# The first channel product by seven block products, with the sums of its weights kept in DRAM

## The chip, the cores and the metric

The kernel runs on one core of one Trainium2 chip. Its time is the device time of one execution in microseconds; the kernel before has a median of 951.89 us over three runs (951.26 to 952.92).

## The reference

Eight batches, eight heads, 576 positions, head size 64. An attention stage makes x (batch, 576, 512), and a mixer works on it:

```python
# attention, for each batch and head
q_d, k_d, v_d = means over 4 neighbouring positions        # 144 positions
out_up    = repeat(softmax(q_d k_d^T / 8) v_d, 4)
out_local = softmax(q k^T / 8 where |i - j| < 4) v
x = out_up + out_local                                      # (576, 512) per batch
# mixer
h  = relu(x^T @ w_tok1) @ w_tok2                            # 576 -> 256 -> 576
u  = x + h^T                                                # (576, 512)
h2 = relu(u @ w_ch1) @ w_ch2                                # 512 -> 1536 -> 512
return u + h2
```

The two products of the last line but one are called the first and the second channel product here; they hold most of the arithmetic.

## The kernel before

**Numbers.** Each factor of a product in the mixer is kept as two float16 parts, a rounded value and its remainder. A product of two such factors is three matmuls (`mm3`, line 119: value by value, value by remainder, remainder by value), accumulated in float32 in a PSUM bank. The names in the profile: `uh` is u as two parts, `CW` and `CX` are the parts of w_ch1 and w_ch2, `c` is a bank of either channel product, `h` the hidden activations as two parts.

**Tiles.** Everything is transposed, so that channels lie on partitions and positions on the free axis. The 576 positions are cut into two chunks of 256 and 320. For a chunk the first product (`first`, line 788) makes 12 tiles of 128 hidden channels, each from four blocks of 128 input channels by three matmuls: 12 matmuls a tile. `first_up` (line 803) takes each tile out of its bank with two instructions: ScalarE writes relu(c) as float16 (line 808), VectorE the remainder (line 810). The second product (`second`, line 813) sums over the 12 hidden tiles into four output tiles, 36 matmuls each, and `second_up` (line 827) adds the scaled result to u and sends it out. Three PSUM banks (`m0` to `m2`) serve both products in turn.

**Scales.** Before a chunk's first product, u is divided by a power of two that depends on its largest magnitude (`scaled`, line 717): a maximum over the tiles, a transpose and a broadcast on TensorE (`um_t`, `um_b`), three small instructions on VectorE, then for each of four blocks one instruction on ScalarE (line 730) and one on VectorE (line 732). So `uh` is ready chunk by chunk.

**Side work.** Attention and the token product (`pooled`, `local`, `mix`) of batch b+1, and the loads of batch b+2 (`ahead`), are put between the channel products of batch b: `tick` in the main loop (lines 932 to 961) lets the side work advance in proportion to the work done. `sd`, `td`, `ad` are scores, transposed exponentials and outputs of the pooled attention, `sc`, `pT`, `av` those of the local one; `x` is its result.

**Order.** Batch 0, its weights and the start of batch 1 are ordered by a planner (`drive`, line 160) from estimated costs, with the list `ORDER` (line 34) as the rule between streams that are ready together. From there the code's order holds, and the scheduler may move instructions of one engine past each other; each engine then runs its list strictly in order. SyncE issues the loads and the output transfers, ScalarE the transfer of the pooled output.

The weights of the first product stay in SBUF as 12 tiles `CW` of two parts, 128 by 512 each, from batch 0 on.

## Time and profile before

| | |
|---|---|
| median of three runs | 951.89 us (951.26 to 952.92) |
| the profiled execution | 952.87 us, of it the span of the trace 951.1 us |
| mean granted TensorE clock | 0.98 of full speed |
| TensorE matmuls busy | 96% of the span |
| VectorE, ScalarE, GpSimd busy | 52%, 35%, 24% |
| moved by DMA | 68.34 MB |

Busy shares are means over stages of different kinds: a start of some 100 us in which weights are converted, then one stretch of about 109 us for each batch, then the last batch, which has no side work beside it. The time column of a group is its busy time; "idle before" names whom the engine waited for. The 1.8 us between the span and the execution's time lie around the trace.

### The profile page before, as it was taken

What the parts mean: (1) busy time and instruction counts of PE and PEld (TensorE: products, weight loads), DVE (VectorE), ACT (ScalarE), POOL (GpSimd) and SP (SyncE); (2) the same over time, 40 slices, a digit from 0 to 9 for tenths busy, and PEclk for the clock granted to TensorE, in tenths of its full rate; (3) what the DMA queues carried; (4) which work ended last, traced back from release to release, by engine and by line L of the source; (5) the groups of instructions that cost most, each with busy time, mean ns of one, the idle gap of its engine ahead of it and who ended that gap; (6) DMA issues with size and microseconds to landing.
All of it is one profiled execution on the core that took longest, in us unless ns stands there. A gap on an engine that the chain in (4) does not pass through costs nothing.

```text
span 951.1 us, 26153 instructions
## 1 busy us (share of the span) xinstructions
PE 910.7 (96%) x11456; PEld 680.7 (72%) x11456; DVE 490.9 (52%) x1189; ACT 334.1 (35%) x732; POOL 232.1 (24%) x361
## 2 busy tenths in 40 slices
PE   8777899999999999999999999999999999999998
PEld 4444688677876788677876787677876778767876
DVE  7899987446552356325653365424563254533221
ACT  3755562424252242314242151423333143422120
POOL 4999941511330003400312004400124000000000
PEclk9977899999999999999999999999999999999999
DMA  9772404610250002600241002500124000000000
GB/s 268 199 264 81 177 21 94 185 45 16 75 159 23 21 18 72 162 16 15 70 139 42 21 17 73 168 8 22 37 71 143 15 16 26 14 1 29 12 12 28
DMA packets 28226, 68.34 MB, mean 72 GB/s; under 512 B 3504, under 2 KB 14000, under 8 KB 26864
## 3 DMA queue, kind: packets, MB, share of 16 engines
q1 hardware_dynamic: 25552, 64.30, 22.4%
q10 hardware_dynamic: 2560, 2.36, 1.0%
q8 instruction: 90, 1.47, 0.6%
q14 instruction: 24, 0.20, 0.1%
HBM read 54.85 MB, written 9.44 MB: 68 GB/s over the span
## 4 chain that ended last, share of the span: by engine, by line
PE 45%; DVE 5%; DMA 2%; ACT 1%; issue 0%; ACTq 0%; POOL 0%; SPq 0%
PE c L121 32%; PE t L121 5%; PE ad L553 2%; DMA vw<-od 2%; PE av L622 1%; PE t L686 1%; PE td L544 1%; PE pT L609 1%; PE sc L586 1%; DVE uh L732 1%; DMA vr<-in_vr_dram 1%; PE sd L525 1%; DVE P L605 1%; DVE xh L664 1%; DVE P L598 0%; DVE r L603 0%
## 5 line engine op out<-in xcount | busy, mean ns | idle before, releaser
L121 PE MATMUL c<-uh,CW 128*128 128x256 f16 (+1 forms) x2304 | 310.0, 286 | 0.0
L121 PE MATMUL c<-h,CX 128*128 128x256 f16 (+1 forms) x2304 | 308.5, 286 | 0.0
L121 PEld LDWEIGHTS <-CW 128*128 128x128 f16 x2304 | 218.1, 98 | 65.6 <-issue 6.7
L121 PEld LDWEIGHTS <-CX 128*128 128x128 f16 x2304 | 220.4, 98 | 56.5 <-issue 0.8
L810 DVE SCALAR_TENSOR_TENSOR h<-c,h 128x256 f16<-128x256 f32 (+1 forms) x192 | 87.4, 455 | 157.1 <-ACT h L808 156.5
L808 ACT ACTIVATE h<-c 128x256 f16<-128x256 f32 (+1 forms) x192 | 78.6, 409 | 189.4 <-PE c L121 188.9
L473 POOL TENSOR_TENSOR vr<-vr 72x256 f32<-72x256 f32 x64 | 49.9, 781 | 369.9 <-DVE vm L470 198.1
L836 DVE SCALAR_TENSOR_TENSOR u<-c,io,u 128x256 f32<-128x256 f32 (+1 forms) x64 | 32.9, 514 | 93.2 <-PE c L121 92.6
L711 ACT ACTIVATE u<-t,down 128x256 f32<-128x256 f32 (+1 forms) x64 | 29.9, 498 | 122.8 <-PE t L121 122.8
L713 DVE TENSOR_REDUCE umx<-u 128x1 f32<-128x256 f32 (+1 forms) x64 | 27.7, 450 | 77.1 <-ACT u L711 77.1
L121 PE MATMUL t<-xh,W 128*128 128x512 f16 (+1 forms) x240 | 61.0, 389 | 3.3 <-DVE xh L664 3.3
L499 POOL TENSOR_TENSOR qs<-qk 128x288 f32<-128x288 f32 x56 | 40.9, 730 | 93.7 <-DMA qk<-in_qk_dram 90.0
L470 DVE TENSOR_REDUCE vm<-vr 72x1 f32<-72x512 f32 x64 | 43.2, 677 | 30.5 <-DMA vr<-in_vr_dram 30.0
L121 PE MATMUL t<-W,hid 128*128 128x256 f16 (+1 forms) x384 | 58.2, 287 | 0.0
L627 ACT ACTIVATE x<-av,up 128x512 f32<-128x512 f32 (+1 forms) x40 | 27.1, 681 | 79.3 <-PE av L622 78.8
L537 ACT ACTIVATE pd<-sd,nmd 72x144 f32<-72x144 f32 x128 | 38.9, 378 | 25.5 <-DVE nmd L532 18.7
L664 DVE SCALAR_TENSOR_TENSOR xh<-x,back,xh 128x512 f16<-128x512 f32 (+1 forms) x40 | 33.7, 843 | 23.1 <-ACT xh L662 22.5
L553 PE MATMUL ad<-vd,ptd 72*72 72x65 f32 x512 | 39.4, 229 | 5.9 <-POOL vd L474 5.8
L553 PEld LDWEIGHTS ad<-vd,ptd 72*72 72x72 f32 x512 | 37.5, 145 | 8.2 <-POOL vd L474 6.7
L121 PEld LDWEIGHTS <-W 128*128 128x128 f16 (+1 forms) x240 | 22.3, 98 | 28.2 <-issue 7.8
L730 ACT ACTIVATE uh<-u,us 128x256 f16<-128x256 f32 (+1 forms) x64 | 29.8, 524 | 34.5 <-DVE us L127 23.9
L121 PEld LDWEIGHTS <-hid 128*128 128x128 f16 x384 | 34.9, 98 | 9.5 <-DVE hid L700 0.7
(129 smaller groups left out, 976.2 us busy)
## 6 DMA issues: line engine op xcount, KB each, us to landing
qk<-in_qk_dram SPq DMA_DIRECT2D x32, 579.0 KB
vw<-in_vw_dram SPq DMA_DIRECT2D x32, 351.0 KB
vr<-in_vr_dram SPq DMA_DIRECT2D x64, 144.0 KB
C_raw<-in_c_dram SPq DMA_DIRECT2D x16, 512.0 KB
out_dram<-u SPq DMA_DIRECT2D x32, 160.0 KB
...
```

Of the source, the lines that this page charges most:

```text
L121: nc.tensor.matmul(ps, lhs(a), rhs(c), start=first and i == 0, stop=last and i == 2, **kw)
L470: nc.vector.tensor_reduce(st.vm[:, i:i + 1], t, axis=AX.XY, op=ALU.max, apply_absolute_value=True)
L473: nc.gpsimd.tensor_add(t[:, 0:2], t[:, 0:2], t[:, 2:4])
L499: nc.gpsimd.tensor_add(two, x[:, :, 0:2], x[:, :, 2:4])
L537: nc.scalar.activation(pd[:, par, g], s[:, par, g], AF.Exp, bias=nm[:, par, g:g + 1], scale=0.125 / 16)
L553: nc.tensor.matmul(ps[:, g, par], pt[:, par, kg, G * g:G * g + G], st.vd[:, kg, 2 * pr + par], start=kg == 0, stop=kg == 1)
L664: nc.vector.scalar_tensor_tensor(xh[:, 1], xf(t), back[:n], xh[:, 0], ALU.mult, ALU.subtract)
L711: nc.scalar.activation(u, ps, AF.Copy, scale=st.down)
L730: nc.scalar.activation(t[:, 0], st.u[ch][c], AF.Copy, scale=s)
L808: nc.scalar.activation(ht[:, 0], ps, AF.Relu)
L810: nc.vector.scalar_tensor_tensor(ht[:, 1], ps, 0.0, ht[:, 0], ALU.max, ALU.subtract)
L836: nc.vector.scalar_tensor_tensor(us[c], banks[c], io, us[c], ALU.mult, ALU.add)
```

## The change

From batch 2 on, the first product is made for a pair of hidden tiles (a and b) and both halves of the positions at once. With A the 2 by 2 blocks of u (position half by channel half; columns of 288 positions, two blocks of 128 channels) and the weights of the pair as 2 by 2 blocks too, seven block products replace eight: a11, a12 and a22 are blocks of u, and s1 to s4 are sums and differences of them (s1 = a21 + a22, s2 = s1 - a11, s4 = a12 - s2, s3 = a11 - a21); they are multiplied by blocks of the weights or by sums of these. Each block product is two blocks of 128 channels by three matmuls of 288 columns, 42 matmuls a pair where there were 48 of 256 and 320.

The four results need partial sums of the seven products. A bank `P` takes a11, is copied (x1), takes s2, is copied (u2), takes s3, is read (m5), takes a22. A bank `R` takes s1, is copied (m5), takes s4. A bank `Q` takes a12. The copies are made by ScalarE, the additions by VectorE, then relu and remainder as before.

The sums of the weights are made in batch 1 by `weight_sums` (VectorE adds the parts, GpSimd subtracts, ScalarE and GpSimd split again), written to DRAM and read back, 0.39 MB for a pair in each batch; one of the four takes the place of a half of the weight tile `b` in SBUF. The sums of u are made on GpSimd once the whole of u is there, with one scale for both halves. The second product goes by output tile, both chunks of a tile after each other. The maxima of v become sums of squares on ScalarE. Buffers change to make room, and `ORDER` and `PX` have other values.

```diff
+    def weight_sums():
+        for p in range(NF // 2):
+            sums.append(dram.tile([128, 3, 2, 256], F16, name=f"sums{p}"))
+        for p in range(NF // 2):
+            fa, fb = C1.fin[2 * p], C1.fin[2 * p + 1]
+            y = {}
+            for n, f, o in (("a1", fa, 0), ("b1", fb, 0), ("a2", fa, 256), ("b2", fb, 256)):
+                yield step("V", 0.42)
+                y[n] = T([128, 256], F32, "tm", f"{n}_{p}")
+                nc.vector.tensor_tensor(y[n], f[:, 0, o:o + 256], f[:, 1, o:o + 256], ALU.add)
...
+            def parts(src, o):
+                nc.scalar.copy(o[:, 0], src)
+                nc.gpsimd.tensor_sub(o[:, 1], src, o[:, 0])
+
+            nc.gpsimd.tensor_sub(y["a1"], y["b1"], y["a1"])
+            nc.gpsimd.tensor_sub(y["b1"], y["b2"], y["b1"])
+            parts(y["a1"], ts12[:, 0])
+            parts(y["b1"], ts3)
+            nc.gpsimd.tensor_sub(y["b2"], y["b2"], y["a1"])
+            parts(y["b2"], ts12[:, 1])
+            nc.sync.dma_start(sums[p][:, 0:2], ts12)
+            nc.sync.dma_start(sums[p][:, 2], ts3)
+            yield step("G", 2.0, ("c1", 1, 1, 2 * p + 1))
+            nc.gpsimd.tensor_sub(y["a2"], y["a2"], y["b2"])
+            parts(y["a2"], fb[:, :, 0:256])
...
+        def mixtures():
+            yield from mixed("s1", A[1][0], A[1][1], ALU.add)
+            s = yield from scale_of(0, st.umx.rearrange("p a c -> p (a c)"))
+            st.ui[1] = st.ui[0]
+
+            def block(name, x):
+                st.uh[name] = T([128, 2, 2, HS], F16, "uh", f"{name}h{b}")
+                for i in range(2):
+                    o = st.uh[name][:, i]
+                    yield step("A", 0.5, *([("h", 1, 1, NF - 1)] if b == 2 else [("h", b - 1)]))
+                    nc.scalar.activation(o[:, 0], x[i], AF.Copy, scale=s)
+                    e = yield step("V", 0.5)
+                    nc.vector.scalar_tensor_tensor(o[:, 1], x[i], s, o[:, 0], ALU.mult, ALU.subtract)
+                make(("uh", b, name), e)
...
+    def product7(st, steps):
...
+        for p in range(NP):
+            fa, fb = 2 * p, 2 * p + 1
+            t123 = T([128, 3, 2, 256], F16, "ts", f"t123_{b}_{p}")
+            nc.sync.dma_start(t123, sums[p])
+            if P is None:
+                P = bank("m0", "P")
+                product(P, "a11", weights(fa, 0), True, False)
+                x1 = plain(P, "x1", "A")
+            Ptag, Qtag = ("m0", "m2") if p % 2 == 0 else ("m2", "m0")
+            h = T([128, 2, 2, S], F16, "h", f"h{b}_{p}")
+            R = bank("m1", "R")
+            product(R, "s1", weights(0, 0, t123, 0), True, False)
+            m5 = plain(R, "m5", "A")
+            product(P, "s2", weights(0, 0, t123, 1), False, False)
+            u2 = plain(P, "u2", "A")
+            Q = bank(Qtag, "Q")
+            product(Q, "a12", weights(fa, 1), True, True)
+            nc.vector.tensor_tensor(x1, x1, Q[:, :HS], ALU.add)
+            leave(x1, 0, 0, h)
+            product(R, "s4", weights(fb, 1), False, True)
+            nc.vector.tensor_tensor(u2, u2, R[:, :HS], ALU.add)
+            leave(u2, 0, 1, h)
+            product(P, "s3", weights(0, 0, t123, 2), False, False)
+            nc.vector.tensor_tensor(m5, m5, P[:, :HS], ALU.add)
+            leave(m5, 1, 1, h)
+            if p + 1 < NP:
+                old, P = P, bank(Qtag, "P")
+                product(P, "a11", weights(fa + 2, 0), True, False)
+                x1 = plain(P, "x1", "A")
+            else:
+                old = P
+            product(old, "a22", weights(fb, 0), False, True)
+            leave(old[:, :HS], 1, 0, h)
...
-            nc.vector.tensor_reduce(st.vm[:, i:i + 1], t, axis=AX.XY, op=ALU.max, apply_absolute_value=True)
+            nc.scalar.activation(dump, t.rearrange("p r c -> p (r c)"), AF.Square, scale=2.0 ** -20, accum_out=st.vm[:, i:i + 1])
...
-        for ch in range(2):
-            while ("uh", b, ch) not in made:
+        if b == 1:
+            for ch in range(2):
...
+                if ch == 0:
+                    work.g = together([weight_sums(), work.g], 2)
+        else:
+            while ("uh", b) not in made or ("sums",) not in made:
                 work.go()
+            g = Run(product7(st, 0))
+            while g.next is not None:
                 g.go()
+                tick(2 * S / 7)
```

In `product7`, `product` is the six matmuls of one block product, `plain` a copy of a bank by ScalarE, and `leave` the ReLU on ScalarE and the remainder on VectorE.

Three places of the order follow. **ScalarE at the start of batch 5.** Before, the eight parts of u, four for each chunk, were followed by the first ReLU of the product:

```order
L730 ACTIVATE uh5_0_0_9243<-u5_0_0_8984,us5_0_9217 128x256
L730 ACTIVATE uh5_0_1_9254<-u5_0_1_9035,us5_0_9217 128x256
L730 ACTIVATE uh5_0_2_9257<-u5_0_2_9089,us5_0_9217 128x256
L730 ACTIVATE uh5_0_3_9260<-u5_0_3_9142,us5_0_9217 128x256
L730 ACTIVATE uh5_1_0_9288<-u5_1_0_9184,us5_1_9284 128x320
L730 ACTIVATE uh5_1_1_9291<-u5_1_1_9193,us5_1_9284 128x320
L730 ACTIVATE uh5_1_2_9294<-u5_1_2_9219,us5_1_9284 128x320
L730 ACTIVATE uh5_1_3_9297<-u5_1_3_9250,us5_1_9284 128x320
L808 ACTIVATE h5_0_0_9327<-c1_5_0_0_9314 128x256
```

Now fourteen parts stand there (two each of a11, s1 and s2 are ahead of these rows), then the copies out of the banks P and R:

```order
L782 ACTIVATE a12h5_9469<-u5_2_9352,us5_0_9430 128x288
L782 ACTIVATE a12h5_9469<-u5_3_9369,us5_0_9430 128x288
L782 ACTIVATE s4h5_9474<-s45_0_9453,us5_0_9430 128x288
L782 ACTIVATE s4h5_9474<-s45_1_9454,us5_0_9430 128x288
L782 ACTIVATE s3h5_9483<-s35_0_9479,us5_0_9430 128x288
L782 ACTIVATE s3h5_9483<-s35_1_9480,us5_0_9430 128x288
L782 ACTIVATE a22h5_9488<-u5_2_9352,us5_0_9430 128x288
L782 ACTIVATE a22h5_9488<-u5_3_9369,us5_0_9430 128x288
L903 COPY x15_0_9516<-P_5_0_9509 128x288
L903 COPY m55_0_9533<-R_5_0_9526 128x288
L903 COPY u25_0_9548<-P_5_0_9509 128x288
L551 ACTIVATE pd6_0_9554<-sd6_0_9519,nmd6_0_9525 72x144 x4
```

The copy of P, which the second block product into P has to wait for, now stands behind all fourteen.

**ScalarE and TensorE in the middle of batch 4's first product.** x5_0 is the attention output of the next batch. Before, ScalarE had these rows around it:

```order
L627 ACTIVATE x5_0_8309<-av5_0_8247,up5_7696 128x2x4x64
L600 ACTIVATE P2_110<-P2_110 128x8x38
L662 ACTIVATE xh5_0_8716<-x5_0_8309,back_126 128x512
L600 ACTIVATE P0_108<-P0_108 128x8x38
L613 COPY pt5_1_8418<-pT5_1_8413 128x512
```

Now it stands among the ReLUs of a pair (h4_3) and ahead of the copy x14_3 of the next pair's bank:

```order
L908 ACTIVATE h4_3_8353<-x14_2_8341 128x288
L641 ACTIVATE x5_0_8459<-av5_0_8412,up5_7822 128x2x4x64
L908 ACTIVATE h4_3_8353<-u24_3_8406 128x288
L614 ACTIVATE P2_112<-P2_112 128x8x38
L908 ACTIVATE h4_3_8353<-m54_3_8398 128x288
L903 COPY x14_3_8520<-P_4_3_8513 128x288
```

TensorE's list at the same place, with the end of s1 and the first row of s2 of that next pair:

```order
L124 MATMUL R_4_4_8574<-s1h4_7881,t123_4_4_8571 128x288
L636 MATMUL av5_0_8412<-vw5_0_7350,pt5_0_8311 32x64 x31
L600 MATMUL sc5_3_8530<-qk5_0_7342 32x38 x8
L600 MATMUL sc5_3_8530<-qk5_1_7344 32x38 x8
L600 MATMUL sc5_3_8530<-qk5_2_7346 32x38 x8
L600 MATMUL sc5_3_8530<-qk5_3_7348 32x38 x8
L124 LDWEIGHTS t123_4_4_8571
L124 MATMUL P_4_3_8513<-s2h4_7890,t123_4_4_8571 128x288
```

The matmul into P_4_3 (s2) comes behind av5_0 and sc5_3 and needs the copy x14_3.

**VectorE in a pair of the last batch.** Where one remainder (line 810) stood for each hidden tile, a pair now has these seven rows:

```order
L937 TENSOR_TENSOR x17_0_12585<-x17_0_12585,Q_7_1_12615 128x288
L941 TENSOR_TENSOR u27_1_12613<-u27_1_12613,R_7_1_12598 128x288
L909 SCALAR_TENSOR_TENSOR h7_1_12597<-x17_0_12585,h7_1_12597 128x288
L945 TENSOR_TENSOR m57_1_12605<-m57_1_12605,P_7_0_12578 128x288
L909 SCALAR_TENSOR_TENSOR h7_1_12597<-u27_1_12613,h7_1_12597 128x288
L909 SCALAR_TENSOR_TENSOR h7_1_12597<-m57_1_12605,h7_1_12597 128x288
L909 SCALAR_TENSOR_TENSOR h7_1_12597<-P_7_0_12578,h7_1_12597 128x288
```

The third add stands behind the other two and one remainder, and it reads the bank that a22 accumulates into.

More of the change, by code (lines that the diff above doesn't have):

```diff
@@ L650, in mix @@
         NT = len(TILES)
-        st.hid, st.acc, banks, umx = [], [], {}, []
+        st.hid, st.acc, banks = [], [], {}
         def xf(t):
@@ L675, in products @@
                 make(("t1", b, t), e)
-            for ch in range(2):
+            for ch, two in WALK[b > 1]:
                 s0, N = CHUNKS[ch]
-                for c in range(4):
+                for c in (2 * two, 2 * two + 1):
                     e = yield step("P", 0.3 + N * 2.6e-3, *(("W", "y", NT + i) for i in range(4)), ("hid", b),
-                                   *([("over", b - 1, 0)] if b and ch == 0 else []), take="" if c % 2 else f"gg>{b}")
+                                   *([("over", b - 1, c - 2)] if b > 2 and c > 1 else []), take="" if c % 2 else f"gg>{b}")
                     if c % 2 == 0:
@@ L726, in scaled @@
+                s = yield from scale_of(ch, st.umx[:, ch])
                 uh = st.uh[ch] = []
@@ L738, in together @@
+        return [splits(), products(), takes(), mixtures() if b > 1 else scaled()]
     def together(todo, most):
@@ L816, in second @@
+    def second(st, banks):
+        b = st.b
+        for c, ch in PATH[b > 0]:
+            s0, N = CHUNKS[ch]
             for k in range(3):
-                e = yield step("P", 12 * N * 0.43e-3, ("C2", 4 * k + 3), ("h", b, ch, 4 * k + 3),
-                               take="" if k else f"m>2{ch}")
+                e = yield step("P", 12 * N * 0.43e-3, ("C2", 4 * k + 3),
+                               *([("h", b, ch, 4 * k + 3)] if b < 2 else []), take="" if k else f"m>2")
                 if k == 0:
```

263 lines of the change are left out of this document (176 added, 87 removed).

## The prediction

> **What bounds the kernel now.** I read the busy shares first, then the busy time by stage (columns: stretch, its length, then busy time and count on PE, PEld, DVE, ACT, POOL, then the granted clock, DMA share and GB/s), then who waits for whom.
>
> ```profile
> PE 910.7 (96%) x11456; PEld 680.7 (72%) x11456; DVE 490.9 (52%) x1189; ACT 334.1 (35%) x732; POOL 232.1 (24%) x361
> 50.00:60.00 10.00, 7.07 (x185) 5.21 (x185) 9.80 (x20) 4.71 (x8) 9.37 (x9) 0.60 0.86 238
> 90.00:100.00 10.00, 6.18 (x39) 3.58 (x38) 9.11 (x17) 4.58 (x10) 9.44 (x8) 0.99 0.57 193
> 437.00:546.00 109.00, 107.46 (x1404) 81.45 (x1403) 52.42 (x135) 36.11 (x82) 19.87 (x37) 1.00 0.20 61
> 655.00:764.00 109.00, 106.03 (x1396) 80.68 (x1393) 50.91 (x125) 34.84 (x79) 19.46 (x37) 1.00 0.19 60
> 873.00:951.00 78.00, 74.74 (x607) 59.14 (x605) 17.69 (x38) 11.78 (x28) 0.00 (x0) 1.00 0.06 20
> ```
>
> From batch 1 on TensorE sets the time: it is idle 1.5 to 3 us of the 109 us that a batch takes, at full clock. The other engines have room: VectorE is busy about half of it and ScalarE a third. Only the first 100 us are different; there VectorE (9.80 of 10) and GpSimd are full and TensorE waits.
>
> ```profile
> ACT h L808 <- PE c L121: 188.9, 146, 17.0
> DVE h L810 <- ACT h L808: 156.5, 135, 2.7
> PE td L544 <- ACT pd L537: 4.1, 6, 0.9
> DVE vm L470 <- DMA vr<-in_vr_dram: 30.0, 24, 4.9
> ```
>
> The list of waits (total us, times, longest) says how TensorE stays busy: ScalarE and VectorE wait for it, and not the other way. A tile of the first product owns one of three banks, and nothing it does next needs the bank back soon. That slack is what the change spends.
>
> **What the seven products save.** The ReLU stands at 887.70 and 889.01 behind twelve 256-column matmuls, at 926.59 and 928.22 behind twelve of 320.
>
> ```profile
> 887.70 0.39 ACT L808 ACTIVATE h<-c 128x256 f16<-128x256 f32 x1 [0.93 <-PE c L121]
> 889.01 0.38 ACT L808 ACTIVATE h<-c 128x256 f16<-128x256 f32 x1 [0.93 <-PE c L121]
> 926.59 0.44 ACT L808 ACTIVATE h<-c 128x320 f16<-128x320 f32 x1 [1.19 <-PE c L121]
> 928.01 19.72 PE L121 MATMUL c<-h,CX 128*128 128x320 f16 x144
> 928.22 0.44 ACT L808 ACTIVATE h<-c 128x320 f16<-128x320 f32 x1 [1.19 <-PE c L121]
> ```
>
> So 1.31 and 1.63 us, 0.109 and 0.136 us a matmul; at 288 columns, halfway, 0.1225 us. A pair of hidden tiles took 2 x (1.31 + 1.63) = 5.88 us and now takes 42 x 0.1225 = 5.15 us (0.735 us a product). Six pairs save **4.4 us a batch, 26.5 us over batches 2 to 7**, if TensorE never waits. The first product ends at 928.01 and the ReLU begins 0.21 us later: that is the lag from TensorE to a reader that I use.
>
> **What they add to ScalarE and VectorE.** (Columns: busy us, mean ns of one, then idle time before.)
>
> ```profile
> L808 ACT ACTIVATE h<-c 128x320 f16<-128x320 f32 x96 | 41.9, 437 | 121.3 <-PE c L121 121.3
> L808 ACT ACTIVATE h<-c 128x256 f16<-128x256 f32 x96 | 36.7, 382 | 68.1 <-PE c L121 67.6
> L810 DVE SCALAR_TENSOR_TENSOR h<-c,h 128x320 f16<-128x320 f32 x96 | 46.9, 489 | 95.0 <-ACT h L808 94.6
> L810 DVE SCALAR_TENSOR_TENSOR h<-c,h 128x256 f16<-128x256 f32 x96 | 40.4, 421 | 62.1 <-ACT h L808 62.0
> L836 DVE SCALAR_TENSOR_TENSOR u<-c,io,u 128x320 f32<-128x320 f32 x32 | 17.6, 549 | 48.9 <-PE c L121 48.5
> L836 DVE SCALAR_TENSOR_TENSOR u<-c,io,u 128x256 f32<-128x256 f32 x32 | 15.3, 478 | 44.3 <-PE c L121 44.1
> L732 DVE SCALAR_TENSOR_TENSOR uh<-u,us,uh 128x320 f16<-128x320 f32 x32 | 16.2, 556 | 3.1 <-ACT uh L730 3.1
> L732 DVE SCALAR_TENSOR_TENSOR uh<-u,us,uh 128x256 f16<-128x256 f32 x32 | 15.8, 517 | 2.0 <-ACT uh L730 1.9
> L730 ACT ACTIVATE uh<-u,us 128x320 f16<-128x320 f32 x32 | 15.8, 552 | 10.9 <-DVE io L835 10.6 <-DVE us L127 0.3
> L600 ACT ACTIVATE P<-P 128x304 f32<-128x304 f32 x32 | 14.6, 457 | 37.7 <-DVE P L598 37.7
> L613 ACT COPY pt<-pT 128x256 f32<-128x256 f32 x8 | 3.0, 371 | 0.6 <-PE pT L609 0.3
> L627 ACT ACTIVATE x<-av,up 128x512 f32<-128x512 f32 x32 | 21.7, 681 | 74.9 <-PE av L622 74.3 <-PE sc L586 0.4
> L470 DVE TENSOR_REDUCE vm<-vr 72x1 f32<-72x512 f32 x64 | 43.2, 677 | 30.5 <-DMA vr<-in_vr_dram 30.0
> L531 DVE TENSOR_REDUCE mxd<-sd 72x4 f32<-72x576 f32 x32 | 23.7, 744 | 2.1 <-PE sd L525 2.1
> ```
>
> At 288 columns: ReLU from a bank 0.41, remainder from a bank 0.455, an add with one bank operand 0.51 (priced as the output update), a remainder from SBUF 0.53, a copy out of a bank 0.40 (between 0.371 at 256 and the ReLU), a ReLU from SBUF 0.48 (between the exponential's 0.457 and 0.552). A pair had four ReLUs and four remainders: ScalarE 1.64, VectorE 1.82 us. Now it has three copies and four ReLUs, 3.05 us, and three adds and four remainders, 3.58 us. Per batch that is 8.5 and 10.6 us more, and 14 blocks of u in place of 8 add some 3 us to each. The eight maxima of v leave VectorE (5.4 us) and cost ScalarE about as much. Both stay under two thirds of 109 us, so neither becomes the bound on average. The cost is in the new waits of TensorE.
>
> **The pair by itself (batch 7).** Let s1 start at 0. The products end every 0.735 us; VectorE's order is add x1, add u2, remainder x1, add m5. Add x1 runs 2.42 to 2.93, add u2 3.15 to 3.66, the remainder to 4.19, add m5 to 4.70. The last product a22 accumulates into the bank that add m5 reads, and would start at 4.41: it waits 0.3 us. A pair takes 5.44 us against 5.88, so batch 7 gains **2.6 us**, not 4.4.
>
> **The start of a batch.** Here is the present one, with 256 columns of u prepared while the other half's second product still runs.
>
> ```profile
> 763.79 1.70 ACT L730 ACTIVATE uh<-u,us 128x256 f16<-128x256 f32 x4 [3.59 <-DVE us L127]
> 766.78 0.38 PE L644 MATMUL um_b<-um_m,ones 1*128 1x1 f32 x2
> 767.09 1.80 PE L121 MATMUL c<-h,CX 128*128 128x320 f16 x12
> 767.83 1.92 ACT L730 ACTIVATE uh<-u,us 128x320 f16<-128x320 f32 x4 [2.34 <-DVE io L835]
> 768.73 1.47 PE L121 MATMUL c<-uh,CW 128*128 128x256 f16 x12
> 770.13 1.20 PE L525 MATMUL sd<-qd 64*72 64x144 f32 x16
> 771.27 1.48 PE L121 MATMUL c<-uh,CW 128*128 128x256 f16 x12
> 773.37 0.69 PE L544 MATMUL td<-ident,pd 72*72 72x72 f32 x8 [0.62 <-ACT pd L537]
> ```
>
> TensorE runs from the second product into the first without a gap and waits once, 0.62 us. ScalarE starts 1.05 us after the um broadcast and needs 0.425 to 0.48 us a block, 0.453 at 288. In the change ScalarE makes all 14 blocks before the copy of x1 that s2 waits for: 1.05 + 14 x 0.453 + 0.40, so s2 starts 7.85 us after the broadcast. Into batch 5, TensorE has 24 matmuls of 320 columns (3.26 us), two score groups (1.14 us, 770.13 to 771.27), a11 and s1 (1.47 us): it is there after 5.95 and waits **1.9 us**. VectorE is later still: 14 remainders, an output update and two 0.744 us maxima stand before the exponentials that td needs, worth about 1.0 us more; less the present 0.62, a start costs 2.3 us. The starts of batches 3, 4 and 6 have the same order. Into batch 2 the broadcast is followed by seven small transposes (0.5 us), a11, s1 and a12 (2.2 us) only: 5.1 us of waiting there. In batch 7, 56 matmuls of the second product stand behind the broadcast, and nothing is waited for.
>
> **One knot in the laden batches.** On ScalarE the attention output x5_0 now stands between the ReLUs of one pair, and the copy of x1 for the next pair behind them. x5_0 waits for av5_0, which TensorE issues after s1 of the next pair; only sc5_3 lies between it and s2, which waits for that copy. ScalarE needs 0.21 + 0.68 (x) + 0.48 + 0.46 (exponential) + 0.48 + 0.40 = 2.7 us; sc5_3 covers 0.71:
>
> ```profile
> 785.93 0.78 PE L586 MATMUL sc<-qk 64*32 64x38 f32 x64
> 786.64 1.48 PE L121 MATMUL c<-uh,CW 128*128 128x256 f16 x12
> ```
>
> That is a **2.0 us** wait in each of batches 2 to 6. In the old order x5_0 falls into the second product, which takes nothing from ScalarE.
>
> **Other waits in laden pairs.** Attention puts some 3 us on TensorE between the products of a pair, which helps, and about as much on VectorE ahead of add m5, which hurts. I bound the sum by 0 (all covered) and by 1 us a pair (a maximum and an add late), and take 0.5, nearer to the bare pair's 0.3: 3.0 us a batch.
>
> **The rest.** The sums of the weights put 24 adds on VectorE, 24 copies on ScalarE and 48 subtractions on GpSimd into batch 1, where all three have room: 0 to 8 us, taken as 1, because ScalarE's copies stand in order before ReLUs. Reading 0.39 MB of sums for each pair is hidden while it has about 6 us (the slot is free after s3 of the pair before last); DMA is 20% busy in these batches. Issued late, each would stop s1 outright. Start-up loses eight maxima from a full VectorE (up to -5.4 us) and runs in another order (5 us either way): -2. The second product has the same matmuls in another order: 0.
>
> **Sum.** Batches 3 to 6: -4.4 + 2.3 + 2.0 + 3.0 = +2.9 each, 11.6. Batch 2: -4.4 + 5.1 + 0.4 + 2.0 + 3.0 = +6.1. Batch 7 -2.6, batch 1 +1, start-up -2. Together +14 us on the profiled execution's 952.87, 967; that execution is 1.0 us above the median of 951.89, so **966 us**.
>
> [...] The two start-up rows show 7.07 us busy at a clock of 0.60 and 6.18 us busy at 0.99: how idle TensorE is does not settle it here. [...]
>
> **The rivals.**
> Covered after all, *faster*, 0.20. If the knot and the laden waits vanish, as waits on ScalarE do now, what is left is the starts' 1.9 x 4 + 5.1, the bare pairs' 0.3 x 6 and the start-up: 952.9 - 26.5 + 12.7 + 1.8 - 2 = 939, median 938. For it: the shares of busy time, and that the waits are short. Against: the order of the knot, which no duration mends.
> Even, 0.07: laden waits near 0 in place of 3.0 each, 952.
> Loads on ScalarE, *slower still*, 0.08. VectorE's 30.0 us of waiting for v move to ScalarE, ahead of copies; two batches' worth at 3.4 us a batch, five times, would add 17: 983.
> The clock, 0.03. [...]
> That the products are not cut is excluded: TensorE's list has 252 in place of 288 a batch.
>
> **How the numbers follow.** The forecast has 0.62 and by itself spans 955 to 982. Faster has 0.20, even 0.07, the two worse cases 0.11. The range 936 to 984 takes in the faster case. Changes under 0.2% (1.9 us) can't be told from none.
>
> **What would show it.** Right: TensorE idle 6 to 10 us a laden batch, waiting for ScalarE's copies (s2) and VectorE's adds (a22); a gap of 4 to 6 us before batch 2's s2; the last batch about 2.6 us shorter. Wrong: batches 2 to 6 under 108 us, or the difference in the first 200 us.

## The result and the profile after

The changed kernel took 984.85 us (median of four runs, 980.41 to 987.86) against 952.4 for the kernel before beside it: slower by a factor of 1.034 (95% interval 1.030 to 1.038), some 32 us. The forecast of 966 had the sign right and less than half of the size; 984.85 lies 0.85 us above the range. The profiled execution took 980.41 us.

The busy line of the page after answers to the first line shown of before:

```profile
PE 898.3 (92%) x11218; PEld 662.2 (68%) x11218; DVE 530.0 (54%) x1263; ACT 426.2 (44%) x1028; POOL 305.8 (31%) x457
```

TensorE is busy 12.4 us less, and the span is 27.5 us longer. Where, the busy time by stretch tells (columns as before), cut at the first product of each batch, of the kernel after:

```profile
215.50:348.05 132.55, 118.28 (x1437) 88.02 (x1435) 63.70 (x152) 51.93 (x136) 61.72 (x96) 0.94 0.25 78
348.05:460.46 112.41, 104.81 (x1344) 78.05 (x1344) 57.81 (x143) 48.96 (x121) 27.74 (x46) 0.97 0.26 79
460.46:572.52 112.06, 104.53 (x1371) 78.03 (x1369) 57.81 (x144) 48.49 (x123) 27.55 (x46) 1.00 0.27 81
572.52:687.34 114.82, 105.62 (x1378) 78.31 (x1376) 60.33 (x147) 50.47 (x129) 28.83 (x47) 1.00 0.25 79
687.34:797.13 109.79, 105.06 (x1361) 78.56 (x1362) 55.49 (x141) 46.42 (x117) 25.73 (x44) 0.98 0.28 82
797.13:907.31 110.18, 104.16 (x1367) 77.82 (x1365) 58.02 (x143) 47.51 (x115) 8.01 (x10) 1.00 0.12 37
907.31:978.60 71.29, 66.85 (x542) 52.61 (x539) 23.62 (x55) 17.18 (x42) 0.00 (x0) 1.00 0.13 42
```

And of the kernel before, batch 1, batches 2 to 6 together, batch 7:

```profile
215.48:327.71 112.23, 109.07 (x1413) 82.22 (x1410) 52.84 (x136) 35.89 (x82) 22.11 (x41) 1.00 0.21 61
327.71:877.01 549.30, 540.39 (x7036) 410.31 (x7036) 258.14 (x664) 183.98 (x417) 79.34 (x148) 1.00 0.17 52
877.01:951.10 74.09, 70.73 (x578) 56.26 (x575) 15.70 (x33) 9.86 (x24) 0.00 (x0) 1.00 0.06 19
```

Up to batch 1 nothing is lost in these two profiles (215.50 against 215.48). **Batch 1 loses 20.3 us** (132.55 against 112.23), though its two products are the old ones; batches 2 to 6 lose 10.0 (559.3 against 549.3), batch 7 gains 2.8. In batch 1 TensorE idles 14.3 us in place of 3.2, and its clock is 0.94: 6% of 132.55 is another 8 us. What is new in batch 1 is the making of the sums of the weights, which I had put at 1 us (six of its 24 additions already run at 67 to 83 us, the rest and all copies from 224 us on), and the first part of batch 2's start, which ends it.

VectorE's and ScalarE's rows of batch 1 around 252 us, after:

```profile
251.52 0.88 DVE L973 TENSOR_TENSOR b<-CW 128x256 f32<-128x256 f16 x1 [1.93 <-POOL CW L980]
252.33 0.48 DVE L878 SCALAR_TENSOR_TENSOR h<-c,h 128x320 f16<-128x320 f32 x1
252.73 0.76 DVE L973 TENSOR_TENSOR a<-CW 128x256 f32<-128x256 f16 x1
253.80 0.42 DVE L575 TENSOR_TENSOR od<-ad,rd 72x256 f32<-72x256 f32 x1
254.25 0.41 ACT L979 CAST ts<-a 128x256 f16<-128x256 f32 x1 [3.08 <-DMA sums<-ts]
```

and TensorE's rows beside them:

```profile
248.74 1.79 PE L124 MATMUL c<-uh,CW 128*128 128x320 f16 x12
254.37 1.09 PE L623 MATMUL pT<-ident,P 128*128 128x128 f32 x4 [3.84 <-DVE od L575]
255.25 3.41 PE L124 MATMUL c<-uh,CW 128*128 128x320 f16 x12
260.36 3.40 PE L124 MATMUL c<-uh,CW 128*128 128x320 f16 x12
264.45 3.43 PE L124 MATMUL c<-uh,CW 128*128 128x320 f16 x24
```

An addition of the sums (L973) waits 1.93 us in VectorE's order until GpSimd gives a buffer back, and another takes 0.76 us where the shortest takes 0.41; behind them stands od, for which TensorE idles 3.84 us. ScalarE's next copy waits 3.08 us for a write to DRAM. Then twelve matmuls take 3.41 us in place of 1.79 until about 264. The clock of these stretches:

```profile
252.00:254.00 2.00, 0.00 (x0) 0.00 (x0) 1.93 (x6) 0.00 (x0) 1.64 (x3) 0.90 0.45 143
254.00:264.00 10.00, 9.63 (x77) 6.59 (x78) 5.47 (x11) 3.67 (x10) 9.30 (x16) 0.51 0.22 79
264.00:266.00 2.00, 2.00 (x68) 1.53 (x44) 0.00 (x0) 0.24 (x1) 2.00 (x4) 1.00 0.56 147
```

One idle stretch of 3.84 us is followed by 10 us at a clock of 0.51. A second idle stretch, 2.91 us, stands at the end of batch 1's first product, behind a copy of the sums that waits for GpSimd in ScalarE's order:

```profile
284.47 0.40 ACT L979 CAST ts<-b 128x256 f16<-128x256 f32 x1 [2.44 <-POOL b L984]
286.46 0.63 PE L623 MATMUL pT<-ident,P 128*128 128x128 f32 x4 [2.91 <-ACT ts L979]
```

A third idle stretch, 2.50 us until 225.50, stands in the kernel without the sums too: TensorE waits there for vm_m, the magnitude of a later batch's values. In the kernel before this wait was 0.3 us.

The slow stretch behind the 3.84 us is 2.6 times as long as the idle one. The idle stretches of 2.50 and 2.91 us were each followed by 3.4 us at a clock of 0.50 and 0.51 (from 226.3 and 287.7), and in the start of batch 2, where no idle stretch is over 1.42 us, the clock was 0.50 for 6.8 us (from 349.2). What sets off a slow stretch, and how long it gets, these traces don't show.

What TensorE waited for from batch 2's first product to batch 7's, after (total us, times, longest):

```profile
PE pT L623 <- DVE P L619: 10.9, 19, 1.2
PE P L124 <- ACT x L903: 4.5, 8, 0.8
PE av L636 <- DMA vw<-od: 4.0, 4, 1.4
PE sc L600 <- ACT x L641: 3.9, 5, 0.8
PE td L558 <- ACT pd L551: 2.3, 4, 0.6
```

and two of these waits in batch 3, one right behind the other:

```profile
501.05 0.77 PE L600 MATMUL sc<-qk 64*32 64x38 f32 x64 [0.78 <-ACT x L641]
502.35 0.65 PE L124 MATMUL P<-s2h,t 128*128 128x288 f16 x4 [0.52 <-ACT x L903]
```

### The profile page after: what moved, and what is told of

Its sections match the earlier page's. It is cut to its first block, busy times and chain, and to the rows that moved or that the text cites. A ratio compares the mean times of both kernels' runs of the same rounds, so it can differ in the third digit from the quotient of the medians.

```text
span 978.6 us, 26351 instructions
## 1 busy us (share of the span) xinstructions
PE 898.3 (92%) x11218; PEld 662.2 (68%) x11218; DVE 530.0 (54%) x1263; ACT 426.2 (44%) x1028; POOL 305.8 (31%) x457
## 4 chain that ended last, share of the span: by engine, by line
PE 64%; DVE 15%; ACT 8%; POOL 6%; issue 4%; DMA 4%; ACTq 0%; POOLq 0%; SPq 0%; DVEq 0%
PE c L124 31%; PE t L124 9%; PE P L124 7%; PE ad L567 3%; PE R L124 3%; DMA vw<-od 3%; PE t L702 2%; ACT pd L551 2%; DVE xh L680 2%; PE td L558 2%; PE Q L124 1%; DVE h L909 1%; PE busy L168 1%; PE av L636 1%; PE sc L600 1%
## 5 line engine op out<-in xcount | busy, mean ns | idle before, releaser
L124 PE MATMUL c<-h,CX 128*128 128x320 f16 (+1 forms) x2304 | 304.2, 287 | 0.0
L124 PEld LDWEIGHTS <-CX 128*128 128x128 f16 x2304 | 223.3, 98 | 64.3 <-issue 3.4
L124 PEld LDWEIGHTS <-CW 128*128 128x128 f16 x1440 | 137.4, 100 | 46.0 <-issue 7.2
L771 POOL TENSOR_TENSOR s<-u,u 128x288 f32<-128x288 f32 x12 | 9.3, 796 | 266.9 <-ACT u L729 266.9
L124 PE MATMUL c<-uh,CW 128*128 128x256 f16 (+1 forms) x576 | 82.6, 296 | 0.2 <-DVE h L878 0.2
L124 PEld LDWEIGHTS <-t 128*128 128x128 f16 x648 | 61.5, 99 | 23.8 <-issue 8.3
L678 ACT ACTIVATE xh<-x,back 128x512 f16<-128x512 f32 (+1 forms) x40 | 29.0, 726 | 39.5 <-PE t L124 37.3
L623 PE MATMUL pT<-ident,P 128*128 128x128 f32 (+1 forms) x160 | 25.7, 286 | 19.4 <-DVE P L619 12.6
L484 ACT ACTIVATE dump<-vr 72x512 uint8<-72x512 f32 x64 | 39.9, 624 | 7.5 <-DMA vr<-in_vr_dram 7.2
L716 ACT ACTIVATE hid<-t 128x512 f16<-128x512 f32 x16 | 9.6, 597 | 73.7 <-PE t L124 65.6
## 6 DMA issues: line engine op xcount, KB each, us to landing
out_dram<-u SPq DMA_DIRECT2D x32, 128.0 KB
```

What stands on the lines that cost most here:

```text
L124: nc.tensor.matmul(ps, lhs(a), rhs(c), start=first and i == 0, stop=last and i == 2, **kw)
L484: nc.scalar.activation(dump, t.rearrange("p r c -> p (r c)"), AF.Square, scale=2.0 ** -20, accum_out=st.vm[:, i:i + 1])
L678: nc.scalar.activation(st.xh[t][:, 0], xf(t), AF.Copy, scale=back[:n])
```

## The experiments

"Start" is the first product of batch 1 in the profiled run, "batch 1" the stretch to the first product of batch 2, "2 to 6" that to batch 7's, all in us; a ratio is to the kernel before on the same chip, with its 95% interval. The starts of the kernels whose sums are not moved ahead of batch 1 lie between 214.8 and 220.9. The runs stood on different chips, and the kernel before had medians of 952.4 to 956.8 beside them, so a difference of two medians is good to a few us only.

| run | median | ratio | start | batch 1 | 2 to 6 |
|---|---|---|---|---|---|
| before | 952.4 | 1 | 215.5 | 112.2 | 549.3 |
| after | 984.85 | 1.0338 (1.0295 to 1.0380) | 215.5 | 132.6 | 559.3 |
| sums_copied | 967.35 | 1.0139 (1.0097 to 1.0180) | 214.8 | 120.3 | 563.0 |
| sums_late | 986.63 | 1.0353 (1.0311 to 1.0395) | 218.8 | 131.4 | 561.2 |
| copy_early | 981.57 | 1.0308 (1.0271 to 1.0344) | 216.7 | 132.5 | 558.5 |
| max_on_dve | 993.04 | 1.0424 (1.0389 to 1.0460) | 220.0 | 136.7 | 562.5 |
| sums_gated | 984.80 | 1.0313 (1.0282 to 1.0343) | 219.7 | 130.8 | 561.4 |
| copy_first | 984.86 | 1.0320 (1.0280 to 1.0360) | 216.2 | 132.4 | 563.9 |
| both | 984.71 | 1.0316 (1.0284 to 1.0347) | 217.2 | 132.5 | 560.2 |
| side30 | 998.66 | 1.0463 (1.0421 to 1.0506) | 218.6 | 132.6 | 570.7 |
| side54 | 983.54 | 1.0292 (1.0265 to 1.0319) | 219.7 | 132.5 | 559.1 |
| sums_pool | 987.71 | 1.0348 (1.0320 to 1.0375) | 217.2 | 136.6 | 564.6 |
| sums_early | 989.69 | 1.0358 (1.0320 to 1.0396) | 237.7 | 119.3 | 561.0 |
| early_all | 988.41 | 1.0342 (1.0317 to 1.0368) | 235.7 | 116.9 | 560.1 |
| pool_alone | 996.39 | 1.0437 (1.0384 to 1.0491) | 220.9 | 138.3 | 560.6 |
| pool_early | 1009.99 | 1.0587 (1.0538 to 1.0635) | 258.3 | 117.7 | 560.3 |
| pool_early_copy | 1006.32 | 1.0548 (1.0491 to 1.0605) | 258.3 | 116.4 | 556.5 |
| dve_alone | 976.57 | 1.0212 (1.0166 to 1.0258) | 217.1 | 128.0 | 559.6 |
| dve_gated | 972.22 | 1.0189 (1.0144 to 1.0234) | 218.3 | 122.0 | 558.9 |
| dve_best | 970.75 | 1.0146 (1.0099 to 1.0194) | 219.9 | 121.5 | 557.9 |

### Whose loss it is: the sums, ScalarE's squares, the start of a batch

**sums_copied.** In place of the whole computation of a pair's sums:

```diff
+            nc.sync.dma_start(sums[p][:, 0], fa[:, :, 0:256])
+            nc.sync.dma_start(sums[p][:, 1], fa[:, :, 256:512])
+            nc.sync.dma_start(sums[p][:, 2], fb[:, :, 0:256])
```

> The changed kernel, but the 18 sums of weights are not computed: three plain blocks of weights per pair are copied to DRAM by DMA instead, so that VectorE, ScalarE and GpSimd have none of that work in batch 1 (the products of batches 2 to 7 then use other weights, with the same instructions). Theory A, the sums' steps stand in the engines' orders ahead of batch 1's own steps and hold TensorE up there: batch 1, 132.6 us from its first product to that of batch 2, falls to 112 to 117 us and the time to 960 to 966 us. Theory B, the time was lost in the waits of batches 2 to 7 or by other work on ScalarE: batch 1 stays over 128 us and the time over 975 us.

Theory A. Batch 1 and the rest of this run:

```profile
214.77:335.07 120.30, 114.00 (x1435) 85.26 (x1433) 49.89 (x134) 43.73 (x110) 31.09 (x53) 0.97 0.22 63
335.07:898.04 562.97, 524.17 (x6818) 390.90 (x6816) 290.13 (x714) 242.56 (x603) 118.19 (x190) 0.99 0.24 72
```

The work of the sums costs 12.3 us in batch 1, and 17.5 us by the medians (2.0% by the ratios). The two profiled executions, the fastest of the changed kernel's four and the slowest of this one's, are 8.6 us apart, so where the rest of the 17.5 lies is not shown. Of the 12.3 us, 8.0 are idle time of TensorE (14.3 against 6.3), and the two waits behind the sums shown above (3.84 and 2.91) are 6.75 of these; the other 4.3 are busy time, with the clock at 0.94 in place of 0.97. Batch 1 came out 3 us longer than expected, and the time 1.4. What is left there, 8.1 us over the kernel before, holds the wait for vm_m again (2.58 us), followed by 6.8 us at half clock (half of that is 2.8% of 120.3 us, about what the mean clock of 0.97 lacks). Without the sums the ratio is 1.0139, 13 us; the forecast without its 1 us for them was also +13, and that the two agree is partly luck, since the terms differ (see "Why the prediction was right and wrong").

**max_on_dve.** The reduction of the value windows of batches 2 to 7 goes back to VectorE, and the scale that is made from it back to the maximum.

```diff
...
-                nc.scalar.activation(dump, t.rearrange("p r c -> p (r c)"), AF.Square, scale=2.0 ** -20, accum_out=st.vm[:, i:i + 1])
+                nc.vector.tensor_reduce(st.vm[:, i:i + 1], t, axis=AX.XY, op=ALU.max, apply_absolute_value=True)
```

> The reduction over the value windows of batches 2 to 7 goes back from ScalarE (0.63 + 0.19 us each, 8 a batch) to VectorE's maximum. Theory A: it isn't what holds batch 1 up; batch 1 stays within 3 us of 132.6 and the time within 976 to 990 us. Theory B in the form that ScalarE's squares, which wait for their DMA ahead of the other steps, delay batch 1 and the laden batches: batch 1 under 125 us and the time 10 us or more shorter.

It got 8 us longer, not shorter, and lies above the ranges of both theories (batch 1 136.7): the squares on ScalarE are a gain, and not what holds batch 1 up. The wait for vm_m stays in this run (2.64 us), so that is not due to the squares; what makes those values come later than in the kernel before isn't shown.

**copy_early** and **copy_first** are about the start of a batch. The first lets the program go on to the first products once a11, s1 and s2 are made:

```diff
-            while ("uh", b) not in made or ("sums",) not in made:
+            while ("uh", b, "s2") not in made or ("sums",) not in made:
...
+                while not may(g.next):
+                    work.go()
```

> Only the order at the start of batches 2 to 7 is changed: the copies of the first bank stand behind the three blocks a11, s1, s2 in ScalarE's order, in place of behind all seven. As I put it on record, the start costs 2.3 us in batches 3 to 6 by that wait and more in batch 2, which would come back in part: 1 to 2 us a batch, the time 968 to 977 us. The rival: the later blocks a12, s4 come later in their turn and TensorE waits for these as long: 979 to 988 us, no change.

981.57 us, and batches 2 to 6 at 558.5 against 559.3: the intervals of the two kernels overlap, so no gain is shown. ScalarE's rows kept their order at the start of batch 3, the copies behind all fourteen blocks; only the product a12 moved ahead of s2. So this run does not test the order either. The second edit, with the first one in it, forces the order by data:

```diff
+            s0 = T([128, 1], F32, "sc", f"us0{b}")
+            nc.vector.scalar_tensor_tensor(s0, st.x1[:, 0:1], 0.0, s, ALU.mult, ALU.add)
+            s = s0
...
```

> The scale of the blocks a12, s4, s3, a22 is made new from the first bank's copy, so that ScalarE takes the copies of the first two banks behind 6 blocks' instructions and not behind 14, in every batch from 2 on. What I put on record as the start's cost (2.3 us in batches 3 to 6, from the wait of s2 for that copy): the product s2 begins about 2 us after the first product in place of 3.9 us, and 1 to 2.5 us a batch are won, 970 to 979 us. The rival: a12 and s4 come later by as much and the wait moves to them; 980 to 988 us.

The rival. TensorE at the start of batch 3 in this run:

```profile
458.95 1.08 PE L124 MATMUL P<-a11h,CW 128*128 128x288 f16 x6
461.19 0.28 PE L124 MATMUL P<-s2h,t 128*128 128x288 f16 x1
463.57 0.28 PE L124 MATMUL Q<-a12h,CW 128*128 128x288 f16 x1 [0.43 <-ACT a12h L782]
466.84 0.90 PE L124 MATMUL P<-s3h,t 128*128 128x288 f16 x6 [0.29 <-ACT u L907]
```

s2 begins 2.2 us after a11, as expected, but a12 and s4 come later by more, and s3 begins 7.9 us after a11; in the changed kernel it does so 6.1 us after (466.54 and 460.46). Batches 2 to 6 lose 4.6 us. Part of it is the edit's own: at this start ScalarE idles 1.20 us ahead of a12 for the scale that VectorE makes anew, so what the order alone would give stays open.

### Where the sums stand

**sums_late.** The first addition of each sum waits in program order for the last first product of batch 1.

```diff
-                yield step("V", 0.42)
+                yield step("V", 0.42, ("c1", 1, 1, NF - 1))
```

> The sums keep all their instructions, but the first of them waits in program order for the last first product of batch 1, so that they run beside its second product (about 45 us, in which GpSimd was idle for 34 us). Theory A, as a matter of order: batch 1 falls to 112 to 120 us and the time to 960 to 968 us, since 6 x 6 us of GpSimd fit into the second product. Theory A as a matter of amount (the sums are needed at batch 2's start and GpSimd's 36 us and the two-way handing of one buffer don't fit): batch 2 begins late, batch 1 over 125 us and the time over 973 us. Theory B: no change, 978 to 988 us.

No change, 986.63 us, but the edit did not do what it says: the scheduler moves what is ready past other instructions, and the sums' first addition still ran at 68.2 us (67.5 in the changed kernel), the last at 284.2. So this run tells nothing of the place.

**sums_gated.** Here the place is forced by data: the copies take a scale of one, made from batch 1's last hidden values.

```diff
...
+                one = T([128, 1], F32, "sc", "one")
+                nc.vector.tensor_scalar(one, ready[1].h7[NF // 2 - 1][:, 1, 0, S - 1:S], 0.0, 1.0, ALU.mult, ALU.add)
...
-                nc.scalar.copy(o[:, 0], src)
+                nc.scalar.activation(o[:, 0], src, AF.Copy, scale=one)
```

> All the sums' instructions stay, with their number and order among themselves, but ScalarE's 24 copies take a scale of one that is made from the last hidden values of batch 1's first product: so they, and what follows them, can only run beside its second product. Theory A, it is the place that costs (waits behind one another in the first product, where ScalarE and VectorE carry batch 1's own steps): batch 1's first product gets as short as with the sums copied (62.8 us), batch 2's first product begins 10 to 13 us earlier against batch 1's start (120 to 123 us), the time 963 to 972 us. Theory A2, the chain itself is too long (one pair of buffers, handed back by the write to DRAM, 6 to 8 us a pair, so 36 to 48 us): what is won in the first product comes back as a wait at batch 2's start or in its products; 976 to 988 us.

A2: the first product of batch 1 gets as short as forecast (59.4 us to the first product of the second, 71.4 before the edit), and the second product gives it back. Its rows at 306 to 311 us:

```profile
306.43 0.51 ACT L984 ACTIVATE CW<-a,one 128x256 f16<-128x256 f32 x1 [8.09 <-POOL a L998]
309.01 0.87 DVE L973 TENSOR_TENSOR a<-CW 128x256 f32<-128x256 f16 x1 [2.74 <-POOL CW L985]
309.80 0.91 DVE L680 SCALAR_TENSOR_TENSOR xh<-x,back,xh 64x512 f16<-64x512 f32 x1
310.76 2.29 PE L124 MATMUL t<-xh,W 64*128 64x512 f16 x5 [2.72 <-DVE xh L680]
```

ScalarE waits 8.09 us for GpSimd, VectorE 2.74 us, and the step that TensorE needs (xh) stands behind VectorE's addition.

**both** puts copy_first and sums_gated together.

> Both edits, the copies of the sums beside the second product and the first banks' copies ahead of four blocks. If both theories hold they add: 948 to 960 us, about the kernel before. If the chain of the sums is too long or the start's wait moves on, 965 us or more.

984.71 us: neither gains, nor do both.

**sums_early.** The sums go beside batch 0's first product, the updated block by way of DRAM:

```diff
+            ts += [T([128, 2, 256], F16, "tm", f"ts{i}_{p}") for i in (2, 3)]
...
+            parts(y["a2"], ts[3])
+            nc.sync.dma_start(back4[p], ts[3])
...
+    def weights_back():
+        for p in range(NF // 2):
+            yield step("S", 0.1, ("c1", 1, 1, 2 * p + 1))
+            nc.sync.dma_start(C1.fin[2 * p + 1][:, :, 0:256], back4[p])
```

> All 18 sums and six updated blocks are still computed, with the same instructions but for GpSimd's and VectorE's order, beside the first product of batch 0 (120 to 215 us, where GpSimd is busy 27.5 of 95.5 us, VectorE 56 and ScalarE 44): the parts get buffers of the mixtures' pool, which is empty then, and the updated block goes to DRAM and comes back by DMA when batch 1 has read the old one. Theory C, batch 1 cannot carry the sums beside batch 2's attention in any place of its own: TensorE has all it needs in 120 to 215 us, so the work is hidden there, batch 1 falls to 118 to 122 us as with the sums copied and the time to 963 to 972 us. The rival, the sums' work costs by its amount wherever it stands: what batch 1 wins is lost ahead of 215 us, 976 us or more.

The rival. Batch 1 falls to 119.3 us, and begins 22 us later. Rows at 122 us:

```profile
122.25 0.87 DVE L974 TENSOR_TENSOR a<-CW 128x256 f32<-128x256 f16 x1 [2.38 <-POOL ts L982]
123.05 0.41 DVE L878 SCALAR_TENSOR_TENSOR h<-c,h 128x256 f16<-128x256 f32 x1
123.51 2.72 PE L124 MATMUL c<-uh,CW 128*128 128x256 f16 x12 [6.25 <-DVE h L878]
```

The same picture in another place: the remainder that TensorE waits 6.25 us for stands behind an addition of the sums that waits for GpSimd. This is one wait of the 22 us; the others are not followed up.

**side30 and side54** change only the pace at which the next batch's attention is put among the products (`SIDE`, 42).

> Only the pace at which the next batch's attention is put among the products is changed (42 to 30 of its units): more of it stands beside the second product, where VectorE and ScalarE are busy 10 to 20 per cent, and less beside the first, where TensorE waits for them 6 to 7 us a batch. Theory A with the laden waits as a matter of crowding: 3 to 8 us fewer over batches 1 to 6, 974 to 982 us. The rival, the readiness of instructions decides the place and not the pace: no change, 982 to 988 us.

> The other direction of the pace: 42 to 54, more of the next batch's attention among the first product. At 30 the time was 14 us longer. If the attention's chain is what comes late for the next batch's start, 54 gives 3 to 8 us, 976 to 982 us; if 42 stands at the best place, 984 us or more.

At 30 neither holds: 998.66 us. Batches 2 to 6 take 11.4 us more; TensorE waits 1.90 us for the um broadcast into batch 3, as if less attention were left to fill the start of a batch, which is not shown further. At 54 the time is 1.3 us less, within the intervals.

**early_all** joins sums_early, copy_early and the pace 54.

> Sums beside batch 0's first product, the order of copies of the earlier run (it measured 3.3 us under the change) and the pace at 54. If the three add: 955 to 966 us; still not under the kernel before, since the start of batch 2 and some 2 us a batch are left. If the pace is no gain: 962 to 970 us.

988.41 us, above both ranges; the loss ahead of batch 1 stays (start 235.7).

### Which engine

**sums_pool.** The 24 copies go from ScalarE to GpSimd (`nc.gpsimd.tensor_copy`).

> The 24 copies of the sums' split go from ScalarE to GpSimd, in the place where the change has them. If it is ScalarE's order (its copies wait for the write to DRAM and for GpSimd, with softmax and relu steps behind them) that holds batch 1 up: 5 to 12 us shorter, 973 to 980 us. If it is the handing between GpSimd and VectorE, or GpSimd's own steps of batch 3's values behind the sums (17 us more on GpSimd): no gain or up to 10 us longer, 984 to 995 us.

987.71 us, batch 1 at 136.6: ScalarE's order alone is not it, though the copies now load GpSimd, which may hide a gain.

**pool_alone** and **pool_early** put all 16 instructions of a pair on GpSimd, in the change's place and early.

```diff
-                nc.vector.tensor_tensor(y[n], f[:, 0, o:o + 256], f[:, 1, o:o + 256], ALU.add)
+                nc.gpsimd.tensor_tensor(y[n], f[:, 0, o:o + 256], f[:, 1, o:o + 256], ALU.add)
-                nc.scalar.copy(o[:, 0], src)
+                nc.gpsimd.tensor_copy(o[:, 0], src)
```

> All 16 instructions a pair of the sums (4 additions, 4 differences, 4 copies, 4 remainders) stand on GpSimd, in the place where the change has them, so that no instruction of VectorE's or ScalarE's order waits for a buffer or a value of the sums; GpSimd has 96 x 0.7 = 67 us of them in place of 35. Theory D, what costs is that an instruction of the sums, waiting in VectorE's or ScalarE's order for another engine, holds up the steps of the batch behind it (in the change VectorE's addition waited 1.93 us at 251.5 us, and TensorE idled 3.84 us for the step behind): batch 1 loses that, but GpSimd's other steps come later; 967 to 980 us. Theory E, the cost is the amount (GpSimd's time, and the slower VectorE beside it): 985 us or more.

> The same on GpSimd alone, beside batch 0's first product (68 us of GpSimd's time were free in 120 to 215 us), with the updated block by way of DRAM. Theory D: no order but GpSimd's holds them, GpSimd's own steps of batch 1 lie behind, 963 to 975 us. Theory E: as with the sums early on three engines, 985 us or more.

Theory D, that it is only the waiting in the other engines' orders, falls: no order but GpSimd's holds a step of the sums now, and the time is 996 and 1010 us. So this waiting isn't the only cause; GpSimd has twice the instructions of the sums now. In the first of the two:

```profile
262.63 0.49 DVE L878 SCALAR_TENSOR_TENSOR h<-c,h 128x320 f16<-128x320 f32 x1 [3.46 <-ACT h L876]
264.77 18.20 DVE L612 TENSOR_TENSOR P<-P,mx 128x304 f32<-128x304 f32 x1
281.83 0.72 POOL L983 TENSOR_TENSOR a<-b,a 128x256 f32<-128x256 f32 x1
283.43 0.96 PE L124 MATMUL c<-uh,CW 128*128 128x320 f16 x3 [15.47 <-DVE h L878]
```

and the same stretch by engine:

```profile
264.77:282.97 18.20, 2.51 (x79) 1.83 (x77) 18.20 (x2) 1.07 (x3) 18.20 (x34) 0.66 0.23 76
```

One subtraction of VectorE's (L612), both inputs in SBUF, 0.47 us at the median in the changed kernel, ran 18.20 us while GpSimd executed 34 instructions without a gap, and TensorE waited 15.47 us for what stood behind it. The remainder at 262.63, with one input in PSUM, took its usual 0.49 us beside the same row of GpSimd's. The changed kernel's profile has the same difference on this tile, P: the subtraction and the multiplication (L619), both inputs in SBUF, took up to 0.95 and 1.40 us, and the addition (L607), one input in PSUM, never over 0.48; the median of each is 0.47. What kept one instruction that long beside GpSimd's row is not shown.

In pool_early the loss has another form as well. TensorE's largest wait from 60 to 360 us:

```profile
PE ad L567 <- POOL vd L488: 30.2, 2, 26.0
```

The values of batch 1's attention stand behind the sums in GpSimd's own order.

**pool_early_copy** adds copy_early to it.

> The one before with the earlier order of products at the start of batches 2 to 7 (which alone measured 3.3 us under the change). Theory D: 960 to 972 us, by 2 to 4 us under the one before. Theory E: 982 us or more.

1006.32 us, 3.7 under pool_early with overlapping intervals.

**dve_alone** and **dve_gated** take GpSimd out of the sums instead, in the change's place and behind the gate of sums_gated:

```diff
-                nc.gpsimd.tensor_sub(o[:, 1], src, o[:, 0])
+                nc.vector.tensor_sub(o[:, 1], src, o[:, 0])
-            nc.gpsimd.tensor_sub(y["a1"], y["b1"], y["a1"])
+            nc.vector.tensor_sub(y["a1"], y["b1"], y["a1"])
```

and so for the other differences.

> GpSimd has no step of the sums: the 4 differences and 4 remainders a pair go to VectorE (0.44 us each, 21 us in all), the additions and ScalarE's copies stay where the change has them. Theory F, taken from the run with all of it on GpSimd, where one subtraction of the softmax with two SBUF inputs (0.47 us elsewhere) ran for 18.2 us beside an unbroken row of GpSimd's instructions: it is GpSimd's row that holds up VectorE's two-input instructions, in the change too (its additions take 0.41 to 1.3 us). Then batch 1 falls to 118 to 125 us and the time to 964 to 975 us. Theory E, the amount of work on the two engines and the handing over between them: VectorE gets 21 us more, and the time is 982 us or more.

> The same without GpSimd, with ScalarE's copies (and so all splits) beside batch 1's second product, where VectorE is busy 17 of 57 us with the sums left out. Theory F: the second product carries 21 to 31 us of VectorE's work with no row of GpSimd's beside it, and loses less than the gated run did on three engines: 962 to 975 us. Theory E, with the copies' waits for the write to DRAM in ScalarE's order: 980 us or more, as gated before (984.8 us).

dve_gated is as Theory F has it; dve_alone lies between the two theories (976.57, over F's 975 and under E's 982; batch 1 128.0 and not 125). By the medians 8.3 us are back in place, 12.6 behind the gate, of the 17.5 (by the ratios 1.3% and 1.5% of 2.0%), though VectorE has more to do. Behind the gate alone (sums_gated, 984.80) nothing was won, so there it is the move from GpSimd that gives it. VectorE's groups of batch 1 (busy us, mean ns of one, idle before), of the changed kernel:

```profile
L973 DVE TENSOR_TENSOR a<-CW 128x256 f32<-128x256 f16 x9 | 5.7, 634 | 9.1 <-POOL ts L980 7.8 <-POOL b L988 1.2
L680 DVE SCALAR_TENSOR_TENSOR xh<-x,back,xh 128x512 f16<-128x512 f32 x4 | 5.1, 1272 | 3.0 <-ACT xh L678 3.0
L619 DVE TENSOR_TENSOR P<-P,r 128x304 f32<-128x304 f32 x4 | 3.7, 924 | 0.0
```

and of dve_gated:

```profile
L973 DVE TENSOR_TENSOR a<-CW 128x256 f32<-128x256 f16 x9 | 4.3, 481 | 0.0
L680 DVE SCALAR_TENSOR_TENSOR xh<-x,back,xh 128x512 f16<-128x512 f32 x4 | 3.7, 916 | 1.8 <-ACT xh L678 1.8
L619 DVE TENSOR_TENSOR P<-P,r 128x304 f32<-128x304 f32 x4 | 2.5, 613 | 0.1
```

The additions, the softmax and the token product's remainder were a third to a half longer in the changed kernel, where GpSimd is busy 61.72 us of batch 1 in place of 34.34, and VectorE's 9.1 us of waiting for it are gone. VectorE is busy 73.60 us in batch 1 of dve_gated, 63.70 in the changed kernel's:

```profile
218.32:340.36 122.04, 113.69 (x1436) 85.90 (x1434) 73.60 (x196) 54.41 (x136) 34.34 (x53) 0.97 0.29 84
```

How the cost divides between longer instructions and handing over isn't shown: these two runs take both away. pool_alone, which has no handing over, shows only that a longer row of GpSimd's is enough to cost as much.

**dve_best** adds copy_early and the mixtures' sums of activations on VectorE.

> The run without GpSimd beside the second product (972.2 us), with two more edits: the mixtures' sums of activations of batches 2 to 7 go from GpSimd to VectorE (8 a batch, 0.44 for 0.79 us; the remainder of s2 beside them took 1.02 us where the other blocks' took 0.51), and the order of copies of the earlier run. If the row of GpSimd's at the start of each batch costs what VectorE's longer instruction shows (0.5 to 1 us a batch) and the order 3 us as alone: 962 to 968 us, still above the kernel before (954 us), by what the copies and additions of the batches cost. If the start is bound by ScalarE's blocks alone: 970 to 974 us.

970.75 us, 1.0146, not told apart from dve_gated (1.0189), and in the range for a start that is bound by ScalarE's blocks. No version came under the kernel before.

## Why the prediction was right and wrong

**The failed step is the price of the weights' sums: 1 us, with 0 to 8 as its bounds; it measured 17.5** (984.85 less 967.35; even the changed kernel's fastest run and the slowest of sums_copied are 8.6 apart). I took it from busy shares ("all three have room"), not from a row, and the upper bound was a guess. The work is a chain over VectorE, GpSimd, ScalarE and a write to DRAM, with few buffers; each link waits in an engine's order ahead of steps that TensorE needs, beside GpSimd's part VectorE's instructions with both inputs in SBUF are longer (an addition 634 ns in the changed kernel's batch 1, 481 in dve_gated's), and the two idle stretches it opens (3.84 and 2.91 us) were followed by 10 and 3.4 us at a clock of 0.51. Of what I had named, only "ScalarE's copies stand in order before ReLUs" was right (the wait of 2.91 us), and it isn't enough (sums_pool).

**Start-up, -2:** measured 0.0 (215.50 against 215.48), where such starts spread over 6 us between runs.

**The saving, 4.4 us a batch:** TensorE's busy time in batches 2 to 6 fell from 540.4 to 524.2 us (the sum of five rows), 16.2 in place of 22; the clock of 0.97 in batch 2 and 0.98 in batch 5 makes up the difference of 5.8 (3% of 112.4 and 2% of 109.8 are 5.6).

**The laden batches, +2.9 each and +1.0 in batch 2 beside its wait (+12.6; +17.7 with that wait, which I had put behind a11 and so into this stretch):** measured +10.0 over the five. "TensorE idle 6 to 10 us a laden batch" nearly holds: 5 to 9 us (length less busy). But its parts are others. The start: I had added up 7.85 and 5.95 us, which are 7.79 and 5.87, with the same 1.9 between them; s2 waits 0.85 us at most for the copy there, in batches 3 and 6, and with the waits beside it a start of batches 3 to 6 costs about 2.0 us, where I had 2.9 before taking off the old 0.62. The knot of x5_0 is there in all five batches, as the two rows of batch 3 show it: sc waits 0.78 us for ScalarE's x and s2 behind it 0.52 for the copy, 1.3 us together, 6.5 in all where I had put 10. In their place TensorE waits 10.9 us for VectorE's softmax (pT; 1.1 in the kernel before), 2.2 us a batch: my "other laden waits", 3.0, were the largest part. The sum came near, its division did not.

**Batch 2's start, 5.1:** a gap, but spread: from 344.0 to 356.0 us TensorE idles 3.8 us, 2.1 of them ahead of the first product, and the clock is 0.50 from 349.2 to 356.0. It was not the one long wait of s2 (0.25 us). What of it lies in batch 1 isn't parted from the sums; without them batch 1 is still 8.1 us longer than before, part of that by the wait for vm_m, which the sum of the prediction didn't have.

**Batch 7, -2.6:** measured -2.8, but not by the bare pair: a pair takes 5.18 us and not 5.44, since a22 doesn't wait (VectorE's add took 0.45 to 0.46 us where I had 0.51). In its place s1 waits 1.13 us once, for VectorE's output update, where I had said that nothing is waited for. That the number fits is luck. **The second product in another order, 0, and the reads of the sums, hidden:** no row after names them as a wait of TensorE's.

**The rivals.** Faster and even are excluded, and neither sign of being wrong came: batches 2 to 6 took 110 to 115 us each, and the first 200 us are as before. The loss in batch 1 was none of the signs that I had named. Loads on ScalarE (983) came near the time by another road: max_on_dve shows that ScalarE's squares save 8 us. The clock did fall, to 0.94 over batch 1, to 0.50 for 6.8 us at batch 2's start and to 0.51 for 3.4 us in batch 5 (from 728.0); a fall over all the laden products is not shown, batches 3, 4 and 6 stand at 1.00.
